# Loads on GpSimd's queue, each begun when the third transfer ahead of it has arrived

## The chip, the cores and the metric

The kernel runs on one core of one Trainium2 chip. The metric is the device time of one execution in microseconds, taken as the median of several runs. The core has four engines that compute, each with its own queue of instructions in program order: TensorE (PE in the profile, PEld for its weight loads), VectorE (DVE), ScalarE (ACT) and GpSimd (POOL). SyncE (SP) issues transfers and does not compute. The core's 16 DMA engines carry all transfers.

## The reference

Two layers follow each other. The first is attention in chunks: for 4 batches and 8 heads, a sequence of 768 positions with 64 numbers each is cut into chunks of 32 queries; each chunk sees 8 memory rows, its own 32 keys, 16 keys to the left and 8 to the right.

```python
for c in range(nc):                      # 24 chunks of 32
    q_c = q[:, :, c_start:c_end]
    k_full = concat([mem_k, k[:, :, l_start:r_end]], axis=2)
    v_full = concat([mem_v, v[:, :, l_start:r_end]], axis=2)
    a = softmax(0.125 * q_c @ k_full.T)
    out[:, :, c_start:c_end] = a @ v_full
```

The second is a mixture of depths. For each batch every position gets a score, the product of its 512 numbers with a gate vector. The 128 positions with the highest scores go through a two-layer network, and its result, times the sigmoid of the score, is added to them.

```python
scores = x @ w_gate                      # x is (4, 768, 512)
top = 128 highest of scores[b]
ye = relu(x[b, top] @ w1) @ w2           # 512 -> 1024 -> 512
out[b, top] = x[b, top] + sigmoid(scores[b, top])[:, None] * ye
```

## The kernel before

The attention is done in 16 pairs of heads, four to a batch; a pair's number is n. For each pair three loads bring k, q and v from memory, casting to 16 bits: LK, LQ and LV, in the function `load`, 96 rows of 2 x 512 numbers or 192 KB each. Each of k, q and v has six buffers (`GB = 6`), so a load of pair n writes the buffer of pair n - 6. The weights of the second layer come in eight more loads, LW.0 to LW.7, of 256 KB each, function `LW`. All of these are issued by POOL. At the start POOL also loads the memory rows of all pairs (PM), and SP copies each pair's rows from there into the pair's buffers (MK and MV, 8 KB each).

Then, for each pair, PE transposes k, q and v into PSUM (TK, TQ, TV, all on L269); a copy on ACT or DVE brings them to SBUF (EK, EQ, EV). Keys need the memory columns in every segment: FK, a copy of kT. Values need the overlap of neighbouring segments: FV and VP, copies of vT. PE then builds the value windows (W0 and W1, L319), the scores (S, L378), the subtraction of the maximum (A, L395), the transposes of the probabilities (PT, L410) and the products (PV, L441). E0 and E1 are the copies of the windows to SBUF, R the maximum, E the exponential, NM the division.

When a batch is done, SP stores its 768 rows in six transfers (ST, L478). The steps whose names begin with m are the second layer of a batch: mGD computes the sigmoid (on POOL, with a reciprocal on DVE in its middle, L526 to L529), mC compares scores (L536), mGI gathers the chosen rows with an indirect transfer on POOL (L601), mGT, mFa, mFb, mYa, mYb are the network on PE, and mSCAT adds the result to memory with another indirect transfer on POOL (L679).

The order of all steps is written out by hand in the string `ORDER`, where each entry is a step, its pair or batch and its engine: `a` ACT, `v` DVE, `g` POOL, `p` PE, `s` SP. Each engine works through its own entries in that order, and an instruction that has to wait holds back all behind it on its engine. Which engine does FK, FV and VP differs from pair to pair. Some parts of the order around POOL's loads read:

```
LV.7.g S.4.p EK.6.a FK.5.g EP0.3.v TV.5.p GP.2.v EP1.3.a FK.6.g
...
LV.9.g VG.4.v R.5.v W0.5.p LW.4.g mR0.0.a PV.4.p mGD.0.g mR1.0.a E0.5.v
...
TQ.7.p LW.6.g EK.7.a PT.5.p RC.4.v mC0.0.v LW.7.g S.6.p
EP0.5.a mC5.0.v mC4.0.v E1.5.a VP.6.g EP1.5.v VG.5.a EQ.7.a NM.4.v W0.6.p W1.6.p
```

The loads with more than one load between them and the next copy are, in POOL's order: LW.1, LW.2, LK.6, then VP.4; LQ.6, LV.6, LK.7, LQ.7, LV.7, then FK.5 and FK.6; LW.3, LK.8 to LV.9, LW.4, then mGD.0; LW.5 to LW.7, then VP.6; LK.10 to LK.14, then mGI.0; LQ.14, LV.14, LK.15, LQ.15, then FV.9 and VP.9; at last LV.15.

Each POOL transfer has one of eight semaphores, in turn, so it also waits until the transfer eight ahead of it has landed.

Of the kernel before, what the change touches and what calls it, by code (L numbers as in the profile page):

```python
# [9 lines left out]
F16 = mybir.dt.float16  # L10
# [61 lines left out]
def _dap(x, offset, dims):  # L72
    return bass.AP(tensor=x.tensor, offset=offset, ap=[list(d) for d in dims])
# [7 lines left out]
def kernel(  # L81
# [13 lines left out]
    nc = tc.nc  # L95
# [15 lines left out]
    GB = 6  # L111
# [3 lines left out]
    def pool(name, bufs, psum=False):  # L115
        return ctx.enter_context(tc.tile_pool(name=name, bufs=bufs, **(dict(space=bass.MemoryType.PSUM) if psum else {})))

    cst = pool("cst", 1)
# [18 lines left out]
    mk16 = cst.tile([4 * NPR, 1024], F16, tag="mk16")  # L137
    mv16 = cst.tile([4 * NPR, 1024], F16, tag="mv16")

    def load(src, dst, p0, n):  # L140
        nc.gpsimd.dma_start(out=dst[n % GB][p0:p0 + 96, :, :],  # L141
                            in_=_dap(src, 2 * n * HD, [[512, 96], [HD, 2], [1, 512]]))

    def LK(n, e):
        load(k, kls, 4, n)

    def LQ(n, e):
        load(q, qls, 0, n)

    def LV(n, e):  # L150
        load(v, vls, 4, n)
# [17 lines left out]
    w1_sb = cst.tile([128, 4, F], F16, tag="w1")  # L169
    w2_sb = cst.tile([128, 8, Dm], F16, tag="w2")  # L170

    def LW(n, e):
        if n < 4:
            nc.gpsimd.dma_start(out=w1_sb[:, n, :], in_=_dap(moe_w1, 128 * F * n, [[F, 128], [1, F]]))
        else:
            o = 2 * (n - 4)
            nc.gpsimd.dma_start(out=w2_sb[:, o:o + 2, :], in_=_dap(moe_w2, 128 * Dm * o, [[Dm, 128], [128 * Dm, 2], [1, Dm]]))
# [499 lines left out]
    def mSCAT(b, e):  # L677
# [4 lines left out]

    cst_cmp = pool("cmp", 6)
    steps = dict(LK=LK, LQ=LQ, LV=LV, MK=MK, MV=MV, LW=LW, C0=C0, C1=C1, C2=C2, CV=CV, CW=CW, CP=CP, CQ=CQ, CZ=CZ, PM=PM, TK=TK, TQ=TQ, TV=TV, EK=EK, EQ=EQ, EV=EV,
                 FK=FK, FV=FV, S=S_, R=R_, A=A_, E=E_, PT=PT, SG=SG, W0=W0, W1=W1, VG=VG, VP=VP,
                 PV=PV, RC=RC, GP=GP, NM=NM, ST=ST, XC=XC, mSC=mSC, mB0=mB0, mB1=mB1, mR0=mR0, mR1=mR1, mGX=mGX,
# [12 lines left out]
    for token in ORDER.split():  # L699
        name, n, e = token.split(".")  # L700
# [36 lines left out]
```

## Time and profile before

| | |
|---|---|
| median of 3 runs | 152.33 us (151.75 to 153.22) |
| the profiled execution's own time | 150.89 us |
| its span, first to last instruction | 149.2 us |
| mean granted TensorE clock | 0.878 |
| busy: PE, DVE, ACT, POOL | 110.2, 94.2, 84.6, 66.2 us |
| transfers of POOL's queue (q0) | 13.55 MB, 58.0% of 16 DMA engines |
| transfers of SP's queue (q1) | 6.54 MB, 12.4% |
| k, q, v loads, median from issue to landing | 7.5, 7.4, 7.2 us |
| weight loads, the same | 9.5 us |

The profile is of one execution. Its page gives busy times, the span in 40 slices, the chain of work that ended last, and groups of instructions. Other views of the same trace list the instructions in order of time with the idle time ahead of each and what ended it, or sum busy time over chosen windows. Times in a view are microseconds from the start of the span. "Issue" in the chain is time in which an engine waited for nothing that the profile shows. In the windows, the clock and the DMA share come after the engines.

### The profile page before, as it was taken

The numbers are of one execution on the slowest core, as the hardware profiler recorded it, in microseconds if no ns is written. First come the engines' busy times: TensorE is split into PE (matmuls) and PEld (weight loads), VectorE is DVE, ScalarE is ACT, GpSimd is POOL, SyncE is SP. The second block draws the span as 40 slices with busy tenths as digits, with TensorE's granted clock in tenths as the row PEclk, the third lists the DMA queues.
The fourth block names the chain that finished last, engine by engine and source line by source line (L and its number), as shares of the span: only waits on it lengthen the run. The fifth ranks groups of instructions, "written<-read, shape, count | busy, mean of one in ns | idle before, by whom it ended". The sixth has DMA issues, their size and how long they took to land.

```text
span 149.2 us, 6550 instructions
## 1 busy us (share of the span) xinstructions
PE 110.2 (74%) x2920; PEld 90.3 (61%) x2920; DVE 94.2 (63%) x207; ACT 84.6 (57%) x139; POOL 66.2 (44%) x119
## 2 busy tenths in 40 slices
PE   0344199984877929697599989989999987799400
PEld 0332198863655819586487867877889676669100
DVE  0771245897169894395447999789798795964000
ACT  3830067973469784606647957979895783412300
POOL 6799069289059591355834014115126027204120
PEclk9999999999599985555559999999999999969975
DMA  2969967969999999999999910501930022365450
GB/s 16 143 69 182 201 107 111 140 90 153 194 180 159 155 286 285 227 209 205 204 242 265 325 38 4 75 4 23 352 130 4 0 77 18 57 255 182 62 70 0
DMA packets 17084, 20.51 MB, mean 137 GB/s; under 512 B 2324, under 2 KB 12564, under 8 KB 17056
## 3 DMA queue, kind: packets, MB, share of 16 engines
q0 software_dynamic: 12832, 13.55, 58.0%
q1 hardware_dynamic: 4224, 6.54, 12.4%
q8 instruction: 23, 0.38, 0.9%
q14 instruction: 5, 0.04, 0.1%
HBM read 24.21 MB, written 7.34 MB: 211 GB/s over the span
## 4 chain that ended last, share of the span: by engine, by line
PE 49%; DMA 15%; issue 15%; DVE 9%; ACT 3%; POOL 3%; POOLq 1%; ACTq 0%; SPq 0%
DMA out_dram<-y,idx 6%; PE p_x L441 5%; PE p_k L269 5%; PE p_v L269 4%; PE p_w L319 4%; PE p_s L378 4%; DMA vl<-mv 4%; PE p_s L395 4%; PE p_v L319 4%; PE p_p L410 4%; PE p_q L269 3%; DMA mv<-in_mem_v_dram 3%; PE p_h L632 3%; DVE m L390 2%; PE p_v L329 2%
## 5 line engine op out<-in xcount | busy, mean ns | idle before, releaser
L127 ACT COPY vT<-p_v 128x800 f16<-128x800 f16 x15 | 12.2, 828 | 14.1 <-PE p_v L269 14.0
L402 ACT ACTIVATE P<-p_s 128x768 f16<-128x768 f32 x16 | 13.0, 815 | 9.6 <-PE p_s L395 7.4
L390 DVE TENSOR_REDUCE m<-p_s 128x12 bf16<-128x768 f32 x16 | 15.2, 952 | 5.1 <-PE p_s L378 5.1
L441 PE MATMUL p_x<-vw,pt 128*64 128x66 f16 (+2 forms) x480 | 12.7, 202 | 4.5 <-issue 1.6
L470 DVE TENSOR_TENSOR x<-p_x,rd 128x768 f32<-128x768 f32 x16 | 15.2, 950 | 0.6 <-PE p_x L441 0.4
L319 PEld LDWEIGHTS <-vT 128*128 128x128 f16 x192 | 13.7, 109 | 2.7 <-issue 0.8
L131 POOL COPY vT<-vT 128x576 f16<-128x576 f16 (+1 forms) x14 | 7.9, 570 | 16.8 <-ACT vT L127 13.6
L441 PEld LDWEIGHTS <-pt 128*64 128x64 f16 x480 | 10.6, 121 | 7.4 <-issue 3.6
L269 PE MATMUL p_k<-rot,kl 100*64 100x100 f16 x256 | 10.8, 243 | 5.6 <-DVE vl L199 5.6
L536 DVE TENSOR_SCALAR cmp<-brow,scr 128x768 f16<-128x768 f32 x24 | 14.3, 642 | 0.5 <-ACT brow L127 0.5
L679 POOL DMA_INDIRECT out_dram<-y,idx x4 | 6.5, 1627 | 17.6 <-ACT y L673 7.5
L378 PE MATMUL p_s<-kT,qT 64*32 64x64 f16 x768 | 9.6, 206 | 6.1 <-issue 4.9
L127 ACT COPY qT<-p_q 128x768 f16<-128x768 f16 x12 | 9.6, 803 | 7.6 <-PE p_q L269 7.6
L269 PE MATMUL p_v<-rot,vl 100*64 100x100 f16 x256 | 10.7, 239 | 4.1 <-DMA vl<-mv 3.3
L269 PE MATMUL p_q<-ident,ql 96*64 96x96 f16 x256 | 10.2, 231 | 4.7 <-issue 2.6
L269 PEld LDWEIGHTS <-kl 100*64 100x64 f16 x256 | 8.7, 135 | 6.4 <-DMA kl<-in_k_dram 5.6
L129 DVE COPY pt<-p_p 64x768 f16<-64x768 f16 x19 | 10.5, 552 | 2.9 <-POOL ltri L242 2.0
L141 POOL DMA_DIRECT2D kl<-in_k_dram x16 | 10.5, 657 | 4.0 <-DMA vl<-in_v_dram 1.3
L378 PEld LDWEIGHTS <-qT 64*32 64x32 f16 x768 | 7.1, 95 | 8.4 <-issue 6.0
L141 POOL DMA_DIRECT2D ql<-in_q_dram x16 | 10.3, 646 | 4.1 <-DMA w_sb<-in_moe_w_dram 2.7
L269 PEld LDWEIGHTS <-ql 96*64 96x64 f16 x256 | 7.9, 126 | 7.0 <-issue 3.6
L269 PEld LDWEIGHTS <-vl 100*64 100x64 f16 x256 | 8.3, 130 | 5.9 <-issue 4.6
(103 smaller groups left out, 253.7 us busy)
## 6 DMA issues: line engine op xcount, KB each, us to landing
out_dram<-x SPq DMA_DIRECT2D x24, 256.0 KB
kl<-in_k_dram POOLq DMA_DIRECT2D x16, 192.0 KB, 7.5
ql<-in_q_dram POOLq DMA_DIRECT2D x16, 192.0 KB, 7.4
vl<-in_v_dram POOLq DMA_DIRECT2D x16, 192.0 KB, 7.2
w_sb<-in_moe_w_dram POOLq DMA_DIRECT2D x8, 256.0 KB, 9.5
vl<-mv SPq DMA_DIRECT2D x15, 8.0 KB
kl<-mk SPq DMA_DIRECT2D x15, 8.0 KB
mk<-in_mem_k_dram POOLq DMA_DIRECT2D x1, 128.0 KB, 5.2
```

What stands on the lines that cost most here:

```text
L127: nc.scalar.copy(out=out, in_=in_)
L129: nc.vector.tensor_copy(out=out, in_=in_)
L131: nc.gpsimd.tensor_copy(out=out, in_=in_)
L141: nc.gpsimd.dma_start(out=dst[n % GB][p0:p0 + 96, :, :], in_=_dap(src, 2 * n * HD, [[512, 96], [HD, 2], [1, 512]]))
L269: nc.tensor.transpose(out=p[64 * h:64 * h + 64, rows * j:rows * j + rows], in_=src[n % GB][0:rows, h, 64 * j:64 * j + 64], identity=perm)
L319: nc.tensor.transpose(out=p.bitcast(F16)[:, 128 * o:128 * o + 128], in_=pair(n, 6 * i + o), identity=ident16)
L378: nc.tensor.matmul(out=s.s[32 * c:32 * c + 32, h, 64 * blk:64 * blk + 64], lhsT=qf[64 * h:64 * h + 64, 32 * ch:32 * ch + 32], rhs=kf[64 * ...
L390: nc.vector.tensor_reduce(out=s.m, in_=keys(s.s), axis=AX.X, op=ALU.max)
L402: nc.scalar.activation(out=s.P, in_=keys(s.s), func=AF.Exp, scale=0.125)
L441: nc.tensor.matmul(out=X[64 * cc:64 * cc + 64, c2, w * (2 * bp + h):w * (2 * bp + h) + w], lhsT=s.PT[:, i, c, :, :].rearrange("p b t -> p ...
L470: nc.vector.tensor_tensor(out=x5.rearrange("p b g (h d) -> p b g h d", d=D), in0=s.x[:, :, :, :, 0:64], in1=s.rd.unsqueeze(4).to_broadcast ...
L536: (nc.vector if e == DVE else nc.gpsimd).tensor_scalar(out=t, in0=m.brow, scalar1=m.scr[:, bl:bl + 1], scalar2=None, op0=ALU.is_lt)
```

## The change

Ahead of each load of k, q, v or weights, a new function `paced` is called with one element of the load's destination, in partition 32. It keeps a list of these elements. From the fourth load on it first issues a copy on POOL of the element that the third load ahead writes, into a small tile `seen`. The copy can only run once that load has landed, and the load itself stands behind the copy in POOL's order. The memory rows, the gathers and the scatters are not in the list, and SP's transfers are as before. With this there are 53 more instructions on POOL, and the other engines have the same instructions in the same order.

```diff
+    seen = cst.tile([33, 1], F16, tag="seen")
+    sent = []
+
+    def paced(dst):
+
+        if len(sent) >= 3:
+            nc.gpsimd.tensor_copy(out=seen[32:33, :], in_=sent[-3])
+        sent.append(dst)
+
     def load(src, dst, p0, n):
+        paced(dst[n % GB][32:33, 0, 0:1])
         nc.gpsimd.dma_start(out=dst[n % GB][p0:p0 + 96, :, :],
                             in_=_dap(src, 2 * n * HD, [[512, 96], [HD, 2], [1, 512]]))
...
     def LW(n, e):
+        paced(w1_sb[32:33, n, 0:1] if n < 4 else w2_sb[32:33, 2 * (n - 4), 0:1])
         if n < 4:
             nc.gpsimd.dma_start(out=w1_sb[:, n, :], in_=_dap(moe_w1, 128 * F * n, [[F, 128], [1, F]]))
```

## The prediction

> **What bounds the kernel now.** I read the page first, then the chain that ended last, then the windows by stage, then the timeline of POOL, whose queue the change edits. The page:
>
> ```profile
> span 149.2 us, 6550 instructions
> ...
> PE 110.2 (74%) x2920; PEld 90.3 (61%) x2920; DVE 94.2 (63%) x207; ACT 84.6 (57%) x139; POOL 66.2 (44%) x119
> ...
> PEclk9999999999599985555559999999999999969975
> DMA  2969967969999999999999910501930022365450
> ...
> q8 instruction: 23, 0.38, 0.9%
> ```
>
> No engine is full over the span. The DMA row is at 9 from slice 9 to 23, roughly 33 to 86 us, and nearly idle after. The chain, in order of time, shows what PE does meanwhile:
>
> ```profile
> 35.29 2.59 issue
> ...
> 42.82 1.07 issue
> ...
> 47.76 1.02 issue
> ...
> 53.16 2.82 issue
> ```
>
> These are stops for which the profile names no producer. The windows between their ends show what they are:
>
> ```profile
> 43.89:48.78 4.89, 3.66 (x128) 2.99 (x128) 4.14 (x10) 4.05 (x7) 4.60 (x8) 1.00 1.01 152
> 48.78:55.98 7.20, 4.38 (x127) 3.75 (x128) 6.70 (x12) 5.46 (x10) 5.41 (x10) 0.92 1.11 223
> ...
> 56.00:82.00 26.00, 22.22 (x561) 18.77 (x561) 14.82 (x34) 13.55 (x24) 11.53 (x18) 0.56 1.21 234
> ...
> 90.00:120.00 30.00, 29.10 (x919) 24.39 (x917) 25.41 (x60) 25.01 (x41) 8.55 (x14) 1.00 0.26 75
> ```
>
> Columns: PE, PEld, DVE, ACT, POOL busy with counts, then clock, DMA share, GB/s. From stop to stop PE and PEld together run 256 instructions, give or take one. Queue q8 brought instructions in 23 packets, and 5840 instructions of PE and PEld over 23 is 254. So I read the stops as PE waiting for its next block of instructions, which travels on the same DMA engines as the loads. One block took 4.9 to 7.2 us under loads, and at a DMA share of 0.26 (1836 instructions in 30 us) 4.2 us. From 56 to 82 the granted clock was also 0.56. The loaded stretch is therefore slow for two reasons that fewer transfers in flight might help. What speaks against the change is POOL's queue, which is in order.
>
> **The change, part by part.** Each load from the fourth on gets a one-element POOL copy ahead of it, which reads the third load ahead, so at most three loads are in flight. Nothing moves between engines and no order changes. Fifty-six loads less three make 53 copies. What one costs as work: the nearest small POOL operations and the present waits are
>
> ```profile
> 0.32 0.10 POOL L718 MEMSET const-float32-0.0<- 128x1 f32 x1 [0.32 <-issue]
> ...
> 50.34 0.19 POOL L528 CAST aux<-gt 128x6 f16<-128x6 f32 x1 [1.56 <-DVE gt L527]
> ...
> 57.12 0.63 POOL L141 DMA_DIRECT2D kl<-in_k_dram  x1 [1.28 <-DMA vl<-in_v_dram]
> ...
> 62.78 0.63 POOL L141 DMA_DIRECT2D vl<-in_v_dram  x1 [2.40 <-DMA w_sb<-in_moe_w_dram]
> ...
> 70.06 0.63 POOL L141 DMA_DIRECT2D vl<-in_v_dram  x1 [0.54 <-DMA kl<-in_k_dram]
> ```
>
> 0.10 to 0.20 us; I take 0.20, as it reads and writes SBUF like the cast. As the last rows show, loads wait for an earlier one already; the wait at 57.12 is for the load begun at 46.8, eight ahead. How long transfers take, each from a look at one load:
>
> ```profile
> L141 POOL DMA_DIRECT2D vl<-in_v_dram x1: 669/669/669, 46.8 to 46.8; - x1
> DMA to landing us min/median/max: 10.0/10.0/10.0
> ```
> ```profile
> L141 POOL DMA_DIRECT2D kl<-in_k_dram x1: 629/629/629, 20.8 to 20.8; - x1
> DMA to landing us min/median/max: 3.2/3.2/3.2
> ```
> ```profile
> L141 POOL DMA_DIRECT2D kl<-in_k_dram x1: 887/887/887, 1.4 to 1.4; - x1
> DMA to landing us min/median/max: 3.9/3.9/3.9
> ```
> ```profile
> L141 POOL DMA_DIRECT2D vl<-in_v_dram x1: 629/629/629, 81.4 to 81.4; - x1
> DMA to landing us min/median/max: 6.3/6.3/6.3
> ```
>
> 46.8 plus 10.0, against the begin at 57.12, is 0.28 us from landing to begin. A load with few companions takes 3.2, the first of the first three 3.9, one beside the stores of finished rows 6.3. I take 3.5 for a load with two companions, between 3.2 and 3.9. A load then begins one round after the third ahead of it began: 3.5 + 0.28 + 0.20 = 3.98 us. The bounds are 3.2 + 0.28 + 0.10 = 3.58 and, with 0.3 for the copy in a busy queue, 3.9 + 0.28 + 0.30 = 4.48. Per load that is 1.33 us (1.19 to 1.49). Weight loads are counted alike. Today's pace, gated by DMA itself, is less: from 62.78 to 70.06 lie six begins, 1.21 us each.
>
> The Trainium skill (DMA: Bandwidth & Descriptors, section on the anatomy of one DMA on the gpsimd path) fits a transfer of this queue as about 2.0 us plus its bytes at 436 GB/s. For 192 KB that is an estimate of 2.45 us, a round of 2.9 and 0.98 per load, and pacing would be free in rate; the 3.2 of the trace disagrees and decides.
>
> The rate is the smaller part. The larger one is what stands behind the loads in POOL's order. These rows are the program's copies and steps that other engines wait for:
>
> ```profile
> 30.64 0.57 POOL L174 DMA_DIRECT2D w_sb<-in_moe_w_dram  x1
> ...
> 41.72 0.35 POOL L131 COPY kT<-kT 128x200 f16<-128x200 f16 x1 [4.36 <-ACT kT L127]
> ...
> 48.53 0.26 POOL L526 TENSOR_SCALAR gt<-gt 128x6 f32<-128x6 f32 x1 [0.29 <-ACT gt L521]
> ...
> 50.84 2.27 POOL L177 DMA_DIRECT2D w_sb<-in_moe_w_dram  x3
> 53.09 0.90 POOL L131 COPY vT<-vT 128x576 f16<-128x576 f16 x1
> ...
> 80.49 0.95 POOL L131 COPY vT<-vT 128x192 f16<-128x192 f16 x2 [3.66 <-ACT vT L127]
> ```
>
> Their consumers, and the stores that share the DMA engines:
>
> ```profile
> 42.32 0.50 PE L378 MATMUL p_s<-kT,qT 64*32 64x64 f16 x42
> ```
> ```profile
> 50.09 0.18 DVE L527 RECIPROCAL gt<-gt 128x6 f32<-128x6 f32 x1
> ```
> ```profile
> 56.46 0.82 PE L319 MATMUL p_w<-ident,vT 128*128 128x128 f16 x6
> ```
> ```profile
> 82.12 0.51 PE L319 MATMUL p_w<-ident,vT 128*128 128x128 f16 x6
> ```
> ```profile
> 47.21 4.07 SPq L478 DMA_DIRECT2D out_dram<-x  x6
> ```
>
> Up to 30.64 loads stand far enough apart that the third ahead has landed. From there:
>
> - LW.0 to LV.7 are ten loads, three rounds from first to last. LV.7 begins at 30.85 + 11.9 = 42.8, and FK.5 (41.72 now) starts at 43.4. Its reader S.5, at 42.32, moves to 43.8: +1.5.
> - After FK.5 and FK.6, LW.3 begins at 44.4. LW.4 is seven loads on, 2 1/3 rounds or 9.3 us. The six stores fall in; one round goes at 6.3 instead of 3.5, which adds 2.8 (none to two such rounds: 0 to 5.6). LW.4 begins at 56.5.
> - mGD.0 behind it starts at 57.1, not 48.53. DVE's reciprocal at 50.09 waits for it, until 57.4, and DVE is in order too: the six compares and the reduction of the next pair stand behind it.
> - LW.5 to LW.7 are one round: LW.7 at 60.5. VP.6 runs from 61.1 to 62.0, and W0.6, at 56.46 now, cannot start before 62.0: +5.5. The 2.82 us stop at 53.16 is inside this wait and covers nothing more.
> - LQ.15 is 17 loads on, 5 2/3 rounds or 22.6 us, plus 0.5 for the gather's issue in between: 83.6. FV.9 and VP.9 end at 85.2, and W0.9, at 82.12 now, starts no earlier: +3.1.
>
> Between W0.6 and W0.9 PE now takes 25.7 us. If it still does, W0.9 is 5.5 late; if fewer transfers in flight bring instructions sooner, up to 2.4 us can be won back until VP.9 holds it. I take 4.5, nearer the former, since the clock row shows half speed there, and new pauses will not raise it. The Trainium skill (same page, section Queues, rings and completion order) says each DMA engine goes round its queues packet by packet, so the depth of one queue would hardly matter to the instruction blocks. By that W0.9 would be 5.5 late and the total 1.0 more; the trace shows 4.2 us a block without loads but none at three in flight.
>
> An early gain is left at nothing: PE waits 3.3 us for the first memory rows, and a shorter queue may shorten it,
>
> ```profile
> PE p_v L269 <- DMA vl<-mv: 3.3, 1, 3.3
> ```
>
> but FK.5 and mGD.0, set by POOL alone, give it back by 43.8. After W0.9 the loads are nearly over, PE is 97% busy from 90 to 120, and nothing shifts but the start.
>
> Sum: the profiled execution took 150.89 (span 149.2, 1.7 around it); plus 4.5 is 155.4. It lies 1.4 under the median of the runs shown, 152.33, whose spread is as large; I add half of that: 156.1, say 156.
>
> **The rivals.**
>
> B, faster. If the round is 3.6 us or less, LW.7 begins at 55.0 (43.1 + 2 1/3 + 1 rounds, no cost for the stores), VP.6 ends by 56.6 and the waits on POOL vanish, while instructions come sooner. The 1122 instructions of 56 to 82 would take 18.3 us at the pace of 90 to 120, a gain of 7.4; half of it, since a full recovery of the clock is not shown, gives 150.9 - 3.7 + 0.7 = 147.9. For it: the 256-instruction stops. Against it: at 8 in flight POOL has slack at mGD.0 of only 1.6 us (48.53 to 50.09). It decides below a round of about 3.7.
>
> C, much slower. Loads beside loads, instruction blocks and stores take 3.9 and more, and two rounds fall in the stores: LW.4 at 46.0 + 10.4 + 5.6 = 62.1, LW.7 at 66.5, VP.6 done at 68, VP.9 at 94: W0.9 is 11.9 late, 163. Halfway between this and the forecast, 160, still belongs to it. For it: 6.3 us beside the stores.
>
> D, no change. The limit of eight gates loads already, and PE's stops absorb what POOL loses: a round of 3.7 to 3.8, W0.6 2 us late, the same won back by W0.9: 151 to 153.5. For it: W0.6 stood behind the 2.82 us stop, so 2.4 us of lateness of VP.6 are free.
>
> **How the numbers follow.** A 0.50 (its own range 153.5 to 159), B 0.22, C 0.15, D 0.13. A measurement of this kernel can tell about 1% from no change. Faster is B, same is D, slower is A and C: 0.22, 0.13, 0.65. The range, 148 to 162, reaches into B and C until about a sixth is left out.
>
> **What would show it.** Right: the median from begin to landing of a load falls from above 7 to under 4.5 us; mGD.0's first step starts near 57 and VP.6 near 61, POOL waiting on DMA ahead of most loads; DVE idles at the reciprocal; W0.9 at 86 to 88. Wrong: VP.6 before 57 (B), or VP.6 late and W0.6 not waiting for it. Whether stops of PE shrink between 62 and 85 tells if depth mattered to the instruction blocks.

## The result and the profile after

The changed kernel takes 176.39 us (median of 4 runs, 175.22 to 176.64) where the kernel before takes 152.73 (4 runs, 151.75 to 153.22): a ratio of 1.162, with a 95% interval of 1.155 to 1.169. The forecast was 156.0, with a range to 162. The direction was right, the size was not: 23.7 us instead of 3.7. Executions more than 1.5% above the fastest of their kernel count in the medians given below but not in the ratios ("none" where too few others are left), and where the profiled execution is one of them its trace is read for order and waits alone.

The page of the profiled execution after (176.29 us), the rows that answer to those shown of before:

```profile
span 174.5 us, 6655 instructions
...
PE 113.4 (65%) x2920; PEld 93.6 (54%) x2920; DVE 93.2 (53%) x207; ACT 85.3 (49%) x139; POOL 75.7 (43%) x172
...
PEclk9999999999789855555997555899999999579985
DMA  3897996787899999998899497004047002408540
...
PE 36%; DMA 34%; DVE 9%; POOL 8%; issue 5%; ACT 2%; POOLq 1%; SPq 0%; DVEq 0%
...
kl<-in_k_dram POOLq DMA_DIRECT2D x16, 192.0 KB, 4.1
ql<-in_q_dram POOLq DMA_DIRECT2D x16, 192.0 KB, 4.1
vl<-in_v_dram POOLq DMA_DIRECT2D x16, 192.0 KB, 4.3
w_sb<-in_moe_w_dram POOLq DMA_DIRECT2D x8, 256.0 KB, 4.7
```

By the medians loads of every kind land sooner after their begin (4.1 to 4.7 us, before 7.2 to 9.5), and the kernel is slower all the same: the DMA row reads 7 to 9 over a longer stretch (39 to 109 us, before 33 to 86), with a 4 in it behind the gather, and DMA now sets 34% of the chain. The chain of work that ended last, in order of time, start and length in us, shows on what:

```profile
34.06 5.33 DMA w_sb<-in_moe_w_dram
...
40.65 4.39 DMA kl<-in_k_dram
...
46.59 4.84 DMA ql<-in_q_dram
...
52.02 7.45 DMA kl<-in_k_dram
...
60.07 3.52 DMA kl<-in_k_dram
...
64.17 4.55 DMA w_sb<-in_moe_w_dram
...
69.30 0.71 POOL w_sb L188
...
70.06 0.67 POOL vT L131
...
70.78 0.82 PE p_w L330 x6
```

Load, copy, load, copy: for 36 us the program's end hangs on one landing after another, and only then does POOL come to VP.6 (70.06) and PE to W0.6 (70.78; before 56.46). The rows of POOL in order of time, with the idle time ahead of each and what ended it:

```profile
43.75 0.18 POOL L146 COPY seen<-w_sb 1x1 f16<-1x1 f16 x1 [0.92 <-DMA w_sb<-in_moe_w_dram]
44.23 0.63 POOL L151 DMA_DIRECT2D vl<-in_v_dram  x1 [0.30 <-issue]
...
48.84 0.64 POOL L131 COPY kT<-kT 128x200 f16<-128x200 f16 x2
...
64.97 0.26 POOL L537 TENSOR_SCALAR gt<-gt 128x6 f32<-128x6 f32 x1
...
92.52 1.11 POOL L612 DMA_INDIRECT xg<-out_dram,idx  x1 [0.46 <-DMA out_dram<-x]
98.75 0.18 POOL L146 COPY seen<-ql 1x1 f16<-1x1 f16 x1 [5.12 <-DMA xg<-out_dram,idx]
...
103.38 0.63 POOL L151 DMA_DIRECT2D ql<-in_q_dram  x1 [0.30 <-issue]
104.06 0.95 POOL L131 COPY vT<-vT 128x192 f16<-128x192 f16 x2
```

Two things to see. Behind a copy that waited, the load starts 0.48 us after the copy's start (43.75, 44.23), of which the copy is 0.18 and 0.30 is a pause. And the copy behind the gather (98.75) waits 5.12 us for the gather to land, though it reads a load. What waits for POOL, from DVE's rows and PE's waits (total, times, longest):

```profile
65.26 0.19 DVE L538 RECIPROCAL gt<-gt 128x6 f32<-128x6 f32 x1 [12.40 <-POOL gt L537]
```
```profile
PE p_w L330 <- POOL vT L131: 17.5, 4, 13.0
PE p_p L421 <- DVE vw L129: 10.7, 1, 10.7
...
PE p_q L280 <- issue: 1.3, 1, 1.3
...
PE p_s L389 <- issue: 1.0, 1, 1.0
```

PE waits 17.5 us for the value copies that stand behind loads, and 10.7 for DVE, which is held at mGD.0's reciprocal. PE's stops with no producer named are fewer: 2.3 us, before 10.9 by the same view (4.9, 2.6, 1.6, 1.1, 0.5 and 0.2). Whether that is a gain of the shorter queue is taken up with the rivals below.

### The profile page after: what moved, and what is told of

It is laid out like the page before. It is cut to its first block, busy times and chain, and to the rows that moved or that the text cites. A ratio compares the mean times of both kernels' runs of the same rounds, so it can differ in the third digit from the quotient of the medians.

```text
span 174.5 us, 6655 instructions
## 1 busy us (share of the span) xinstructions
PE 113.4 (65%) x2920; PEld 93.6 (54%) x2920; DVE 93.2 (53%) x207; ACT 85.3 (49%) x139; POOL 75.7 (43%) x172
## 4 chain that ended last, share of the span: by engine, by line
PE 36%; DMA 34%; DVE 9%; POOL 8%; issue 5%; ACT 2%; POOLq 1%; SPq 0%; DVEq 0%
DMA kl<-in_k_dram 12%; DMA w_sb<-in_moe_w_dram 6%; DMA ql<-in_q_dram 5%; PE p_x L452 5%; PE p_h L643 4%; DMA xg<-out_dram,idx 3%; DMA out_dram<-y,idx 3%; PE p_w L330 3%; PE p_v L330 3%; PE p_s L406 3%; DVE x L481 3%; DMA vl<-in_v_dram 3%; DMA out_dram<-x 3%; PE p_p L421 3%; PE p_v L280 2%
## 5 line engine op out<-in xcount | busy, mean ns | idle before, releaser
L330 PEld LDWEIGHTS <-vT 128*128 128x128 f16 x192 | 14.3, 113 | 20.9 <-POOL vT L131 18.0
L330 PE MATMUL p_w<-ident,vT 128*128 128x128 f16 x96 | 9.8, 251 | 18.3 <-POOL vT L131 17.5
L421 PE MATMUL p_p<-ident,P 128*128 128x128 f16 x96 | 9.8, 250 | 10.7 <-DVE vw L129 10.7
L127 ACT COPY pt<-p_p 64x768 f16<-64x768 f16 x13 | 10.3, 793 | 12.3 <-PE p_p L421 11.7
L452 PE MATMUL p_x<-vw,pt 128*64 128x66 f16 (+2 forms) x480 | 13.6, 210 | 2.6 <-DVE scp L475 1.1
L452 PEld LDWEIGHTS <-pt 128*64 128x64 f16 x480 | 11.7, 130 | 5.5 <-issue 2.4
L547 DVE TENSOR_SCALAR cmp<-brow,scr 128x768 f16<-128x768 f32 x24 | 13.5, 607 | 1.2 <-ACT brow L127 1.1
L421 PEld LDWEIGHTS <-P 128*128 128x128 f16 x96 | 7.3, 112 | 11.5 <-issue 10.7
L280 PEld LDWEIGHTS <-kl 100*64 100x64 f16 x256 | 8.1, 127 | 9.5 <-DMA kl<-in_k_dram 8.8
L129 DVE COPY vw<-p_w 128x768 f16<-128x768 f16 x10 | 5.4, 545 | 13.3 <-PE p_w L330 12.9
```

Of the source, the lines that this page charges most:

```text
L127: nc.scalar.copy(out=out, in_=in_)
L129: nc.vector.tensor_copy(out=out, in_=in_)
L280: nc.tensor.transpose(out=p[64 * h:64 * h + 64, rows * j:rows * j + rows], in_=src[n % GB][0:rows, h, 64 * j:64 * j + 64], identity=perm)
L330: nc.tensor.transpose(out=p.bitcast(F16)[:, 128 * o:128 * o + 128], in_=pair(n, 6 * i + o), identity=ident16)
L421: nc.tensor.transpose(out=p[:, 128 * i:128 * i + 128], in_=s.P[:, h, 2 * bp:2 * bp + 2, :].rearrange("p b k -> p (b k)"), identity=ident16)
L452: nc.tensor.matmul(out=X[64 * cc:64 * cc + 64, c2, w * (2 * bp + h):w * (2 * bp + h) + w], lhsT=s.PT[:, i, c, :, :].rearrange("p b t -> p ...
```

## The experiments

Three theories. P: the loss is place; what stands behind paced loads in POOL's in-order queue comes late, and with it the engines that read it. R: the loss is rate; three transfers in flight bring the rows too slowly, whatever the queue. I: the copies as instructions take POOL's time. The "fourteen steps" are VP.0, VP.1, FK.1, FV.1, VP.2, FV.3, VP.4, FK.5, FK.6, mGD.0, VP.6, FV.9, VP.9 and mGD.1. The marks W0.6, W0.9 and W0.10 are the starts of PE's value windows in each profiled execution, in us; ratios are to the kernel before on the same chip, with 95% intervals. The kernel before took 150.2 to 153.5 us by its medians on these chips, so times of different rows are best compared by the ratios.

| run | W0.6 | W0.9 | W0.10 | median | ratio |
|---|---|---|---|---|---|
| before | 56.5 | 82.1 | 89.3 | 152.73 | 1 |
| after | 70.8 | 105.1 | 114.0 | 176.39 | 1.162 (1.155 to 1.169) |
| eight in flight | 56.9 | 84.3 | 92.4 | 152.12 | 1.011 (1.001 to 1.020) |
| five | 59.2 | 88.7 | 97.9 | 155.26 | 1.030 (1.021 to 1.040) |
| four | 61.6 | 90.2 | 98.6 | 161.67 | 1.062 (1.028 to 1.095) |
| three, gather later | 71.5 | 104.0 | 112.5 | 173.80 | 1.155 (1.145 to 1.165) |
| three, steps off POOL | 56.8 | 80.7 | 103.4 | 165.24 | 1.104 (1.095 to 1.113) |
| the same, gather earlier | 57.9 | 86.7 | 95.1 | 163.22 | 1.067 (1.057 to 1.078) |
| those moves, no copies | 58.8 | 78.5 | 85.8 | 153.00 | none (149.27 to 154.78) |
| copies early only | 70.4 | 94.8 | 101.4 | 164.33 | 1.082 (1.070 to 1.093) |
| copies late only | 55.5 | 93.9 | 103.0 | 168.55 | none (166.25 to 171.32) |
| early only, steps off POOL | 56.4 | 82.9 | 101.4 | 160.60 | 1.054 (1.034 to 1.073) |
| late only, off POOL, gather earlier | 57.7 | 81.5 | 89.4 | 158.72 | 1.048 (1.041 to 1.055) |
| four, gather later | 63.6 | 91.0 | 100.8 | 161.80 | 1.058 (1.048 to 1.068) |
| five, gather later | 58.3 | 83.8 | 95.7 | 159.66 | none (156.75 to 160.88) |
| five, off POOL, gather later | 56.7 | 80.0 | 93.6 | 152.17 | 0.994 (0.986 to 1.003) |
| eight, off POOL, gather later | 59.5 | 79.9 | 86.8 | 149.09 | 0.991 (0.987 to 0.995) |
| those moves, no copies | 59.0 | 79.0 | 87.1 | 147.88 | 0.976 (0.969 to 0.984) |

Two runs that move the stores are told at their place.

**How many in flight.** The same copies, with another distance:

```diff
-        if len(sent) >= 3:
-            nc.gpsimd.tensor_copy(out=seen[32:33, :], in_=sent[-3])
+        if len(sent) >= 8:
+            nc.gpsimd.tensor_copy(out=seen[32:33, :], in_=sent[-8])
```

> The copies stay, but each reads the load eight ahead, which the load waits for anyway: at most eight in flight, as before the change. Three theories of the 23.7 us. P, place: what costs is that POOL's program copies stand in order behind loads that begin one landing of the third ahead after another; without the narrow window that goes, and only the copies' own work stays, 48 x 0.18 us, mostly in POOL's idle time, plus the wait of the copy behind the gather of the chosen rows. P expects 153 to 157. R, rate: with three in flight the transfers themselves come too slowly and PE waits for data; R expects the same 153 to 157 here. I, the inserted instructions: the copy with its 0.30 us pause ahead of each load is the cost, whatever it reads; I expects above 165.

With eight the copies are there and seldom wait: 1.1% slower, 152.12, just under the 153 to 157 of P and R. So I does not carry the 16%.

> Five in flight instead of three. A round for five is about 5.2 + 0.6 us, 1.16 us a load, which is the pace of the kernel before (1.21). R, rate: the rate is restored, so nearly all of the loss goes: 153 to 156. P, place: the rate is restored but the steps behind LW.7 still wait for three more landings than before (3 x 1.2 us) and for the gather: 157 to 162.

With five, 3.0%. The time, 155.26, lies in R's range (153 to 156) and below P's (157 to 162), though PE's longest wait is still the one that P names: W0.9 stands 9.0 us for a copy of vT on POOL.

> Four loads in flight instead of three, nothing else. The round is then about the latency of 4.7 plus 0.6 for the gate, 5.3 us over four loads, 1.33 per load against 1.57 with three in flight and against 1.0 to 1.2 with eight. With three it was 16% over the kernel before, with five 3%, with eight 1%. P and R alike: W0.6 between 60 and 65, the whole 157 to 163, ratio 1.04 to 1.08. If the step from 3 to 5 is a threshold and not a slope, it is near 154 or near 172.

With four, 161.67, inside what was expected: a slope, not a threshold. This run is worth more than its time, because its pace per load is the forecast's. POOL's rows:

```profile
41.78 0.63 POOL L151 DMA_DIRECT2D vl<-in_v_dram  x1 [0.30 <-issue]
...
43.28 0.57 POOL L185 DMA_DIRECT2D w_sb<-in_moe_w_dram  x1
...
55.71 0.72 POOL L188 DMA_DIRECT2D w_sb<-in_moe_w_dram  x1 [0.29 <-issue]
56.51 0.26 POOL L537 TENSOR_SCALAR gt<-gt 128x6 f32<-128x6 f32 x1
...
60.16 0.72 POOL L188 DMA_DIRECT2D w_sb<-in_moe_w_dram  x1
60.92 0.66 POOL L131 COPY vT<-vT 128x576 f16<-128x576 f16 x1
...
79.11 1.11 POOL L612 DMA_INDIRECT xg<-out_dram,idx  x1 [0.46 <-issue]
85.74 0.18 POOL L146 COPY seen<-kl 1x1 f16<-1x1 f16 x1 [5.52 <-DMA xg<-out_dram,idx]
...
88.52 0.63 POOL L151 DMA_DIRECT2D ql<-in_q_dram  x1
```

From LW.0 (29.73) to LV.7 (41.78) nine loads go at 1.34 us each; the forecast had 1.33. LV.7, LW.3, LW.4, mGD.0, LW.7, VP.6 and W0.6 were forecast for 42.8, 44.4, 56.5, 57.1, 60.5, 61.1 and 62.0; here they are 41.8, 43.3, 55.7, 56.5, 60.2, 60.9 and 61.6. At its own pace the forecast's walk through POOL's queue is right to about 1 us. Then it departs: LQ.15 at 88.5 instead of 83.6, behind 6.6 us from the gather's begin to the end of the copy's wait.

**The wait behind the gather.** mGI.0 moved behind LQ.15, ahead of FV.9, with three, four and five in flight:

```diff
-... EK.9.a mGI.0.g TQ.9.p ...
+... EK.9.a TQ.9.p ...
-... mB1.1.p FV.9.g ...
+... mB1.1.p mGI.0.g FV.9.g ...
```

> Window of three, but the gather of batch 0 (mGI.0) stands behind LQ.15, just ahead of FV.9, instead of behind LK.14. In the changed kernel the copy behind the gather waited 5.12 us, until the gather had landed. If that wait is a part of the loss, it goes from the path of VP.9, and PE waits at most 1.5 us more for the gathered rows: 171 to 174. If the POOL queue would have waited for landings in those 5 us anyway: 175.5 to 177.

> Four in flight and the gather mGI.0 behind LQ.15. With four in flight alone, LQ.15 began at 88.5 against 83.6 in the forecast, W0.9 at 90.2 and the whole was 161.7. If the wait behind the gather is the difference, LQ.15 begins at 81 to 84 and W0.9 at 84 to 87. What of it reaches the end is less certain, as the gather lands later for PE's mGT.0, which stands behind W0.9: 156 to 159 if W0.9 decides (P), 160 to 163 if the gather's landing or the rows of the last loads do.

> Five in flight, and the gather mGI.0 moved behind LQ.15, just ahead of FV.9. With five in flight alone it was 3% over the kernel before, and its gather held the loads behind it for 6 us. If that wait is most of the 3% (P): 150 to 153, ratio 0.99 to 1.01. If the rate is (R): 154 to 156, ratio 1.02 to 1.03 as without the move.

Worth little: 1.155 against 1.162 with three, 1.058 against 1.062 with four, with intervals that overlap; with five 159.66, above both ranges that were expected. (173.80 with three lies in the range for a part of the loss, but on a chip where the kernel before took 150.40.) With four, LQ.15 came at 87.75, where 81 to 84 was expected if the gather were the difference. The likely reason: the stores of the second batch, which begin at 87.96 with three and 78.67 with four and had fallen on the gather's wait, now fall on loads (with three those from 88.81 to 98.80 begin 2.5 us apart). With five W0.9 is 5 us earlier, and PE then waits 2.9 us for the gathered rows, which come later. The copy's wait is real, and with three and four in flight it is not what makes the time.

**Place.** The fourteen steps go from POOL to DVE, three in flight, all copies kept:

```diff
-... VP.0.g ... FK.5.g ... mGD.0.g ... VP.6.g ...
+... VP.0.v ... FK.5.v ... mGD.0.v ... VP.6.v ...
```

> Window of three, but the 14 program steps that stand between the paced loads on POOL (VP.0, VP.1, FK.1, FV.1, VP.2, FV.3, VP.4, FK.5, FK.6, mGD.0, VP.6, FV.9, VP.9, mGD.1) run on DVE, at their places in the order. P, place: nothing that another engine waits for is left behind a paced load except the data; LK.6 would land 3.6 us later than TK.6 began before, the rest in time: 154 to 160. R, rate: PE still waits for the data: above 168.

W0.6 is back at 56.8 (70.8 with them on POOL), at the same pace of loads, and W0.9 at 80.7. So the first 14 us of the loss are place, and not that rows of k, q or v were missing. The whole, 165.24, lies between P's range (154 to 160) and R's (above 168). What it still loses, it loses mostly at the next thing that stands behind loads, by PE's waits of this run:

```profile
PE p_e L619 <- DMA xg<-out_dram,idx: 13.7, 1, 13.7
```

The gather begins at 92.63 behind twelve paced loads. It was moved too, right behind LK.10, with the loads LQ.10 to LK.14 after it, and the same moves were run without copies:

> As e4_off_pool (window of three, the 14 program steps on DVE), and the gather of batch 0 begins right behind LK.10 instead of LK.14. In e4 PE idled 13.7 us for the gathered rows, since the gather itself stands behind twelve paced loads though its index was ready at 68.6 and it began at 92.6. P, place: that wait goes, and what is left is data that lands late: 153 to 158. R, rate: the paced loads behind it still come too late and PE waits for them in place of the gather: 161 to 165.

> Control for the last: the same moves (14 steps on DVE, gather behind LK.10) in the kernel before the change, no copies, eight in flight. The moves alone, both theories: 148 to 153.

163.22, 6.7% slower, in R's range (161 to 165). The moves alone gave 153.00 (149.27 to 154.78) beside 152.21 of the kernel before, no difference that these four runs can show. Of the 16.2% this leaves 6.7, or more if the moves gain something, for rate and for what place remains. By PE's waits and the chain,

```profile
PE p_v L280 <- DMA vl<-in_v_dram: 9.1, 4, 6.7
PE p_w L330 <- POOL vT L131: 6.3, 1, 6.3
```
```profile
72.66 4.36 DMA xg<-out_dram,idx
```

it lacks rows of v, and a value copy, FV.11, that was left on POOL, behind LV.15 and the first scatter. But the long wait for v, 6.7 us, is no wait for rate alone: it is for LV.10, which stands right behind the gather and LQ.10. The copy ahead of LQ.10 waited for the gather until 77.14, so that LV.10 began at 78.46, beside the stores of the second batch (begun from 75.36 on), and landed after 6.8 us. Without copies the same order has LV.10 at 72.05, 1.8 us behind the gather's begin, and PE waits 1.8 us for it. So this run does not show a share of R.

**Which half.** Copies only up to LW.7, or only from LK.10 on:

```diff
-        if len(sent) >= 3:
+        if 3 <= len(sent) < 38:        # late only: if 38 <= len(sent) < 99:
```

> The changed kernel with the copies ahead of the loads up to LW.7 alone; from LK.10 on loads go without. P, place: VP.6 is late as in the changed kernel (W0.6 14.3 us late there), and the later part wins some back, as more loads can be in flight and POOL gets ahead: 160 to 168. If the lateness were from the later loads: below 157.

> The other half: copies ahead of LK.10 and all later loads, none ahead of the first 38. Between W0.6 and W0.9 the changed kernel lost 8.6 us more; by P about this remains: 156 to 162. If one half alone suffices for the whole loss, above 168.

> Copies ahead of the loads up to LW.7 only, and the fourteen steps VP.0, VP.1, FK.1, FV.1, VP.2, FV.3, VP.4, FK.5, FK.6, mGD.0, VP.6, FV.9, VP.9 and mGD.1 on DVE instead of POOL. With the copies alone this half cost 12 us (164.3). Place in POOL's queue (theory P): W0.6 starts near 57 and the whole takes 152 to 156, since nothing early stands behind a load any more and the gather stands behind loads that go as before. Rate of transfers (theory R): the early loads go as slowly as in the run with copies alone, PE waits for the rows themselves, W0.6 near 65 and 160 or more.

> Copies from LK.10 on only, the fourteen steps on DVE, the gather mGI.0 right behind LK.10 and the twelve loads LQ.10 to LK.14 behind it. With the copies alone this half cost 16 us (168.6, W0.9 at 93.9). Place (P): 153 to 157, W0.9 near 80. Rate (R): the loads of the second half still land at 1.57 us each, PE waits for rows of k, q and v, 160 or more.

Early only costs 12.1 us by the medians (152.21 beside it), as P expected; late only 16.3, and by its four times 14 to 19, more than P's range allows (156 to 162, measured 168.55). Together that is more than the 23.7 of the whole, so the two overlap; the likely reason is that what makes PE late in the first half gives POOL time in the second. Late only, PE's one long wait is for POOL:

```profile
PE p_w L330 <- POOL vT L131: 15.4, 1, 15.4
```

With the steps on DVE, early only keeps P's mark (W0.6 at 56.4, expected near 57) but not P's time: 160.6, which only R had. PE's waits say why:

```profile
PE p_e L619 <- DMA xg<-out_dram,idx: 9.7, 1, 9.7
PE p_k L280 <- DMA kl<-in_k_dram: 9.2, 2, 5.0
```

The gather, again behind late loads, and k's rows themselves: here R has its share. Late only with the gather ahead (158.72) lies between the two ranges:

```profile
PE p_v L280 <- DMA vl<-in_v_dram: 6.5, 1, 6.5
...
PE p_w L330 <- POOL vT L131: 5.3, 1, 5.3
```

Again LV.10, which begins at 74.51 because the copy ahead of LQ.10 waited for the gather until 73.20, and again FV.11. Without copies the first of these waits is the 1.8 us named above.

**The stores.** The six stores of the first batch later in SP's queue, three in flight:

```diff
-... mB1.0.p ST.0.s EP0.4.v ...
+... LV.13.g MK.13.s ST.0.s FV.8.v ...        # second try; first: behind MV.11
```

> Three in flight as in the changed kernel, and the six stores of the first batch begun behind MV.11 in SP's queue, past LW.7. The forecast's store term was 2.8 us between LW.3 and LW.4, measured as the difference of 14.1 us there and two and a third rounds of 4.7, 11.0. If the stores are the cause, LW.3 to LW.4 takes 10.5 to 11.5 us, mGD.0 begins near 62 and W0.6 near 67. The loads beside the stores' new place are then slower by as much, so the whole is 173 to 177. If the weight loads beside them were the cause, LW.3 to LW.4 stays above 13.

The first try told nothing: behind MV.11 the stores still began at 49.99 (50.22 in the changed kernel), since SP had done what stood ahead of them by then. LW.3 to LW.4 took 14.1 us as before, 174.92 in all.

> Three in flight as in the changed kernel, and the six stores of the first batch behind MK.13 in SP's queue, so that they begin past 73 instead of 50. If the stores are what makes the loads after LW.3 slow (landing 5.5 to 8.6 us after their begin instead of 4): LW.3 to LW.4 takes 10.5 to 11.5 us instead of 14.1, mGD.0 begins near 62, W0.6 near 67, and the loads beside the stores' new place are slower instead; the whole 172 to 176. If not, LW.3 to LW.4 stays at 13 to 14 and W0.6 near 70.8.

The second moved them by 7 us only, not past 73, so by its figures it could not tell (13.6 us from LW.3 to LW.4, W0.6 at 71.7); the landings do. SP's row in the changed kernel, then here:

```profile
50.22 4.62 SPq L489 DMA_DIRECT2D out_dram<-x  x6
```
```profile
57.26 4.75 SPq L489 DMA_DIRECT2D out_dram<-x  x6
```

In the changed kernel the load begun at 52.02 lands after 7.45 us and the one begun at 60.07 after 3.52 (the chain above). Here the chain has

```profile
51.65 5.46 DMA kl<-in_k_dram
...
57.71 5.90 DMA kl<-in_k_dram
```

and the view of the one load begun at 59.93 (v) gives

```profile
DMA to landing us min/median/max: 7.5/7.5/7.5
```

The slow landings went with the stores: in the changed kernel the loads begun from 52.02 to 56.17 take 6.1 to 8.6 us, here those begun from 57.71 to 59.93 take 5.9 to 7.5. Both places lie between LW.3 and LW.4, so a gain could not show: 176.47 (172.64 to 177.94).

**A version without place.** The fourteen steps on DVE and the gather behind LQ.15, with five in flight, with eight, and without copies:

> Five in flight, the gather moved behind LQ.15, and the fourteen steps on DVE. P: nothing that PE needs stands behind paced loads any more, and what is left is the copies' own time (1% with eight in flight): 149 to 153, ratio 0.98 to 1.01. R: 154 to 156. DVE has 63% of its time busy before and gets 10 us more, so a loss of 1 to 2 us by DVE is possible in both.

> No copies: the kernel before with the gather mGI.0 behind LQ.15 and the fourteen steps on DVE, the control of the run with five in flight and the same moves, which stood at 0.994 of the kernel before. If pacing with five in flight costs nothing and gains nothing once place is gone: ratio 0.985 to 1.00 here too. If the moves gain and the pacing costs (R): 0.96 to 0.98. If the pacing gains: above 1.00.

> The copies with eight in flight, which is the limit that the transfers have anyway, with the gather moved behind LQ.15 and the fourteen steps on DVE. Without copies these moves gave 0.976 of the kernel before, with five in flight 0.994. If the copies cost nothing as instructions and the limit of five is the 1.8% (rate, R): 0.97 to 0.985. If the copies as instructions are the 1.8% (I): 0.99 to 1.00.

Five in flight, 3% slower with everything in its old place, now stands at 0.994, inside what P expected; the moves without any copy, 0.976, beat both kernels, as R expected (0.96 to 0.98). Eight and five in flight lie 1.5 and 1.8 points above that, and by their intervals no difference between them is shown: by the times, what is left when place is gone comes with the copies, as I expects, and not with the limit. The traces do not bear that out, though. The windows of the last stretch, first without copies, then with eight (us, busy time of PE, PEld, DVE, ACT and POOL with counts, clock, DMA share, GB/s):

```profile
118.07:146.00 27.93, 16.44 (x284) 13.09 (x282) 12.08 (x29) 8.06 (x17) 7.00 (x8) 0.84 0.39 95
```
```profile
117.93:147.70 29.77, 18.26 (x285) 14.24 (x282) 12.19 (x29) 8.07 (x17) 7.02 (x8) 0.80 0.36 89
```

The last pair's window starts within 0.14 us in both; the 1.8 us lie behind it, where no copy is left, at a lower granted clock. So up to the last copy these two executions are level, and that the 1.5 points are the copies' price is not shown.

## Why the prediction was right in direction and wrong in size

W0.9 was forecast 4.5 us late and came 22.9 late. Of the 18.4 us between, 8.8 arise up to W0.6 and 9.6 from W0.6 to W0.9; another 2.4 come after it. By the prediction's own steps:

- **The round, 3.98 us: the step that failed.** Measured from LW.0 (34.06) to LV.7 (its begin, 48.17), three rounds: 4.70 us each, 1.57 per load, above even the upper bound of 4.48. The latency was taken as 3.5, "between 3.2 and 3.9" from loads with little beside them; three in flight all the time gave 4.1 to 4.3. From landing to the load's begin were forecast 0.48 (0.28 and 0.20); it is 0.60: 0.12 to the copy's start, 0.18 for the copy, 0.30 pause. The Trainium skill's fit for one transfer of this queue (DMA: Bandwidth & Descriptors, anatomy of one DMA on the gpsimd path) gave an estimate of 2.45 us; with three in flight 4.1 to 4.3 were measured.
- **"Up to 30.64 loads stand far enough apart": wrong.** The gate waits 3.34 us at 13.83 already: the loads three apart that begin at 8.33, 14.30, 18.39 and 23.22 are rounds of 4.1 to 6.0 us, and LW.0 begins at 34.06 instead of 30.85. The timeline of before could have told: there LK.1 to LV.3, nine loads, begin 0.7 us apart (8.14 to 13.77).
- **The walk from LW.0 to W0.6: right.** FK.5, mGD.0, DVE's reciprocal, VP.6 and W0.6 come in the order and through the waits that were named. W0.6 is 14.3 us late instead of 5.5. Of the 8.8 between, 3.2 are LW.0's late start, 2.2 the rounds to LV.7, 0.3 there to LW.3, 2.0 the stretch to LW.4 and 1.1 the last round; four in flight, at the pace assumed, met the marks.
- **The stores, 2.8 us: right, as far as the runs tell.** LW.3 (50.06) to LW.4 (64.17) took 14.1; two and a third of the rounds of 4.70 make 11.0, so about 3.1 are left for the stores, and moving them moved the slow loads. No run has this stretch without them.
- **W0.6 to W0.9, forecast 24.6 us, measured 34.3: the second failure.** I let PE's own pace set this stretch and VP.9 only bound it from below. The window of after, then of four in flight, W0.6 to W0.9:

```profile
70.78:105.06 34.28, 19.18 (x522) 16.48 (x522) 16.21 (x36) 14.47 (x25) 16.14 (x37) 0.65 0.90 161
```
```profile
61.63:90.20 28.57, 19.16 (x522) 16.43 (x522) 16.92 (x38) 14.47 (x25) 15.62 (x37) 0.68 1.04 190
```

  PE has the same 19.2 us of work in both and idles for the rest. Its clock is not what holds it: granted were 0.65, before 0.56 from 56 to 82. LW.7 to LQ.15 is what sets the stretch: 34.1 us (69.30 to 103.38), of which the gather's begin to LQ.14's takes 6.7 (92.52 to 99.25), which the sum had at 0.5, and the 17 loads the other 27.4, 1.61 each instead of 1.33. But where the gather's wait was taken away, with three and four in flight, W0.9 came 1 us earlier or no earlier at all.
- **"Nothing shifts but the start" after W0.9: wrong by 2.4 us.** The last stretch of before, then of after:

```profile
82.12:149.20 67.08, 53.54 (x1381) 43.46 (x1377) 45.35 (x102) 39.00 (x68) 16.84 (x24) 0.93 0.34 93
```
```profile
105.06:174.50 69.44, 56.56 (x1377) 46.59 (x1377) 43.35 (x98) 38.45 (x66) 17.66 (x26) 0.87 0.31 76
```

  Nearly the same count of instructions at a granted clock of 0.87 instead of 0.93. W0.9 is 22.9 late, this adds 2.4, and 150.89 plus both is 176.2; the profiled execution took 176.29. These are two single executions, and the one before lies 1.8 us under its kernel's median, so part of the 2.4 may be chance; for that difference the forecast had added 0.7.
- **The copies, nearly nothing: nearly right.** 1.1% with eight in flight.
- **The rivals.** B needed a round below 3.7 and D one below 3.8; both fall with the round. C had the right mechanism, a longer round, and still stopped at 163, with 4.48 and the early loads left alone. The gain that B hoped for is not shown. PE's stops without a named producer fell from 10.9 to 2.3 us, and with three in flight and the steps on DVE they were 3.0 (1.5, 0.7, 0.4, 0.4); but they follow how long PE stands for other things, and not the depth. Five in flight has 2.4 us of them (1.4, 1.0) with the steps on POOL and 9.3 (4.4, 2.2, 1.4, 1.3) in the version without place; there eight has 9.5 (5.3, 1.7, 1.3, 0.8, 0.4) and no copies 10.6 (4.4, 2.2, 1.6, 1.2, 1.2). A likely reason is that the blocks come while PE waits for something else. That depth hardly matters to the blocks, as the prediction drew it from the Trainium skill (DMA: Bandwidth & Descriptors, queues, rings and completion order), agrees with these runs from eight to five; for three no run has PE free of other waits.

What stays open: why the copy behind the gather waits for the gather (it does so in every trace that has both, whichever load it reads, while FV.9's copy right behind the moved gather does not: with three in flight the gather begins at 101.82 and FV.9 at 102.98); how the 6.7% that remain without most of place divide between rate, that wait and the copies left on POOL; and where the 1.5 points with copies at eight in flight lie. Three in flight with the steps on DVE and the gather behind LQ.15, which would tell most about rate, was not run.

## What to carry to other kernels

Before a wait is put on an engine that issues loads, list what else stands in that engine's queue: a limit on transfers in flight delays all of it, and here moving fourteen steps to another engine, and the gather forward, took back more than half of what the limit of three cost, and without any copies ahead of the loads those steps on DVE, with the gather later, made the kernel 2.4% faster. Price such a gate by latency as it is with that many in flight, plus the whole path from landing to the next begin; per load, latency over depth must stay under the pace that the consumers need, and 53 gated loads three deep can carry an error in a round up to some eighteen times. Landing times that fall are no gain: 7.5 to 4.1 us came with a kernel 16% slower.

## What the runs showed of the hardware

The 0.30 us between the end of a one-element POOL copy that had waited and the start of the next load stood in nearly every round; I had counted nothing for it. With three loads in flight a 192 KB load lands 4.1 to 4.3 us after its begin by the medians, with four 4.5 to 5.4, with five 5.0 to 5.4 and with eight 7.0, all in the old order. The pace does not gain by it: from LW.0 to LK.14, 33 loads on, a load begins every 1.22 us before (30.64 to 70.93), 1.23 with eight (30.74 to 71.48), 1.35 with five (29.81 to 74.48), 1.46 with four (29.73 to 78.02) and 1.74 with three (34.06 to 91.43), POOL's other waits included. And with three in flight a 192 KB load that begins beside six stores of 256 KB took 5.9 to 8.6 us to land instead of about 4, in the changed kernel and in the run that moved the stores by 7 us.
